# Six Strassen pairs in the last two blocks, activation tables loaded at launch, one state copy split over two engines, and a reordered head

## The chip, the cores and the metric

The kernel runs on one core of one Trainium2 chip. The metric is the device time of one launch in microseconds. Every kernel was executed several times, and executions of the kernel before ran on the same chip between them. All executions quoted here are in the fast state with a mean granted clock of 0.99 to 1.00 (the granted clock is the share of its full clock that the tensor engine was given), but for one of 306.76 us of the kernel before, which was slow (over 1.5% above that kernel's fastest) and is left out of the ratios.

## The reference, cut to what matters

```python
def reference(q, k, v, w_in, w_out):        # q, k, v: 8 batches x 8 heads x 576 x 64, f32
    scores = q @ k.transpose(0, 1, 3, 2) / sqrt(64)
    gamma  = 1 - 2.0 ** (-5 - arange(8))                    # one decay per head
    ret    = scores * where(rel >= 0, gamma ** rel, 0)      # rel = i - j
    x      = (ret @ v).transpose(0, 2, 1, 3).reshape(4608, 512)
    h      = x @ w_in                                       # 512 -> 2048
    g      = 0.5 * h * (1 + tanh(c * (h + 0.044715 * h ** 3)))
    return g @ w_out                                        # 2048 -> 512, f32
```

## The kernel before

The retention ("attention") part is computed in chunks of 128 positions, with a running state between chunks. The FFN works in **blocks** of 512 rows. Each of the eight batches gives one block (its first 512 positions), and the last 64 positions of all batches together make a ninth, the tail block. They run in the order 0, 1, 2, 3, 4, 5, 6, tail, 7, so the "last two blocks" are the tail block and block 7. While a block's FFN runs, the attention of the next batch is woven between its matmuls. A block has three parts that matter here. The code below is cut, and cuts are marked.

```python
def bank(name, dt=F32):                       # eight PSUM banks, shared by everything
    return ps.tile([128, 512 if dt == F32 else 1024], dt, tag="bank", name=name)

# inside class Block
def up(self, f):                              # one of 16 columns of 128 of the first FFN
    hp = bank("hp")
    # ... x is xt (tail block) or xb[b]
    for ct in range(4):                       # 4 matmuls of 512, contraction 4 x 128
        nc.tensor.matmul(hp, w_in_sb[:, ct, 128 * f : 128 * f + 128], x[:, :, ct, :],
                         start=(ct == 0), stop=(ct == 3))
    nc.scalar.activation(out=self.g(f // 2)[:, f % 2], in_=hp, func=AF.Gelu_apprx_tanh)

def mix_sa(self, j, n):  # ... three DVE mixes of g: the operands of a Strassen-type
def mix_sc(self, j, n):  # ... second FFN (seven products my, mz, mw, mv, mu, my2, mz2)
def mix_d(self, j, n):   # ... all of them tensor_tensor with both inputs in SBUF, f16

def down(self, m):                            # 16 matmuls of 256, then the sums on DVE or ACT
    self.product(m)
    self.settle(m)
```

The second FFN is thus already done by one Strassen level; the first is not. Around the blocks stand a list of loads, a list of filler matmuls, and one long plan that says behind which unit of PE work each other step is put:

```python
def gelu_table():                             # loads the gelu table, somewhere in the head
    nc.scalar.activation(out=p2[:, 3:4], in_=p2[:, 2:3], func=AF.Gelu_apprx_tanh)

def put(b, n, eng=None):                      # copies the running state n to f16, two halves
    w = att[b]["w", n]
    for hl in range(2):
        copy(eng or nc.scalar, tbd[b % 2][half[hl], n, :, half[hl]], w[half[hl]])

load_qkv(0, 0, 0, "k", None)                  # (batch, half, head group, which, buffer)
load_qkv(0, 0, 0, "q", None)
# ... some 80 further entries, mostly loads of 256 KB, all in one queue: inputs, w_in, w_out, next inputs

pads.update({("tr", 0, 0, 1, 0): 29, ...})    # filler matmuls that keep PE's clock up
plan = add({},
    (0, L(mask)),
    (0, L(tbd_zero, 0, V)),
    (0, L(cast_qk, 0, 0, 0, "k", A)),         # (unit of PE work, step); A, V, G: engine
    (4, L(gelu_table)),
    # ... some 330 further entries
    (78, L(put, 4, 3)),
)
run(units, plan)
```

Of the kernel before, what the change touches and what calls it, by code (L numbers as in the profile page):

```python
# [19 lines left out]
def kernel(  # L20
# [66 lines left out]
    nc.vector.memset(wz, 0.0)  # L87

# [34 lines left out]
    nc.scalar.activation(out=gt, in_=lg[:, 8:12], func=AF.Exp, bias=0.0, scale=128.0)  # L123

# [7 lines left out]

    def gelu_table():
        nc.scalar.activation(out=p2[:, 3:4], in_=p2[:, 2:3], func=AF.Gelu_apprx_tanh)
# [150 lines left out]
    def cast_w_in(g, ct, eng):  # L285
        t = w_raw.pop(("i", g, ct))
        copy(eng, w_in_sb[:, ct, 512 * g : 512 * g + 512], t)
        done(t)

# [162 lines left out]
    def put(b, n, eng=None):  # L452
        w = att[b]["w", n]
        for hl in range(2):
            copy(eng or nc.scalar, tbd[b % 2][half[hl], n, :, half[hl]], w[half[hl]])
# [76 lines left out]
    class Block:  # L532
        def __init__(self, b):
            self.b = b
            self.gT = self.sa = self.sc = self.ost = None
            self.bank = {}
# [23 lines left out]

        def up_half(self, j, u):
# [19 lines left out]
        def mix_sa(self, j, n):  # L581
# [3 lines left out]
            nc.vector.tensor_tensor(  # L585
# [3 lines left out]
        def mix_sc(self, j, n):  # L589
# [3 lines left out]
            nc.vector.tensor_tensor(out=self.sc[:, j : j + n], in0=g[:, :, 0], in1=g[:, :, 1], op=ALU.add)  # L593

        def mix_d(self, j, n):
            g = self.g(j, n)
            nc.vector.tensor_tensor(  # L597
# [133 lines left out]
    def add(plan, *entries):  # L731
# [13 lines left out]
    load_qkv(0, 0, 1, "k", None)  # L745
    load_qkv(0, 0, 1, "q", None)
    load_qkv(0, 0, 0, "v", None)
# [6 lines left out]
    load_qkv(0, 1, 0, "v", None)  # L754
    load_qkv(0, 1, 1, "v", None)
    load_w_in(0, 0, E)
    load_w_in(0, 1, E)
    load_w_in(0, 2, E)
# [4 lines left out]
    load_qkv(1, 0, 1, "q", None)  # L763
    load_qkv(1, 0, 0, "k", None)
    load_w_in(1, 2, E2)
    load_w_in(2, 3, None)
    load_w_in(2, 0, None)
    load_w_in(2, 1, None)
# [3 lines left out]
    load_qkv(1, 0, 0, "v", None)  # L772
    load_w_in(3, 1, None)
    load_w_in(3, 3, None)
    load_qkv(1, 1, 0, "k", O)
    load_w_in(3, 2, None)
    load_qkv(1, 0, 1, "v", None)
    load_qkv(1, 1, 1, "k", O)
    load_qkv(1, 1, 1, "q", O)
# [5 lines left out]
    load_w_out(6, E3)  # L785
    load_w_out(3, None)
    load_w_out(2, None)
# [3 lines left out]
    load_w_out(14, H)  # L791
    load_w_out(13, H)
    load_w_out(7, E3)
    load_w_out(8, O)
    load_w_out(11, H)
    load_w_out(9, O)
# [3 lines left out]
    load_qkv(2, 0, 0, "q", None)  # L800
    load_qkv(2, 1, 0, "k", None)
    load_qkv(2, 0, 0, "k", None)
    load_qkv(2, 1, 0, "q", None)
    load_qkv(2, 0, 0, "v", None)
    load_qkv(2, 0, 1, "k", None)
    load_qkv(2, 0, 1, "q", None)
    load_qkv(3, 0, 1, "k", None)
    load_qkv(2, 0, 1, "v", None)
    load_qkv(2, 1, 1, "k", None)
    load_qkv(2, 1, 0, "v", None)  # L810
    load_qkv(2, 1, 1, "v", None)
    load_tail(0)
    load_qkv(3, 0, 0, "k", None)
    load_qkv(3, 0, 0, "q", None)
    load_qkv(3, 0, 0, "v", None)
# [13 lines left out]
        ("tr", 0, 1, 0, 0): 1,  # L829
        ("tr", 0, 1, 1, 0): 4,  # L830
        ("tr", 0, 1, 1, 1): 5,
        ("st", 0, 1, 0): 0,
        ("st", 0, 1, 1): 6,
        ("us", 0, 0): 0,
        ("us", 0, 1): 11,
        ("xs", 0, 0): 5,
        ("xs", 0, 1): 0,
        ("in", 0, 3): 0,
        ("tr", 0, 0, 0, 0): 5,
        ("tr", 0, 0, 0, 1): 12,  # L840
        ("tr", 0, 0, 1, 0): 29,
        ("tr", 0, 0, 1, 1): 1,
        ("st", 0, 0, 0): 6,
        ("st", 0, 0, 1): 0,
        ("us1", 0, 0): 8,
        ("tr", 0, 1, 0, 1): 8,
        ("in", 0, 1): 10,
        ("us1", 0, 1): 0,
        ("in", 0, 2): 5,
# [6 lines left out]
    def turn():  # L856
# [7 lines left out]
    plan = add({},  # L864
        (0, L(mask)),
        (0, L(tbd_zero, 0, V)),
        (0, L(cast_qk, 0, 0, 0, "k", A)),
        (0, L(cast_qk, 0, 0, 0, "q", V)),
        (4, L(gelu_table)),
        (0, L(tr, 0, 0, 0, 1, S2)),  # L870
        (1, L(score_mm, 0, 0, 0)),
        (0, L(tr, 0, 0, 0, 0, A)),
# [459 lines left out]
```

## Time and profile before

| | kernel before |
|---|---|
| time, median of 3 at first | 302.81 us (302.34 to 303.06) |
| span of the profiled execution | 299.4 us, an execution of 301.22 us |
| PE, DVE, ACT, POOL busy | 97%, 73%, 55%, 27% |
| first batch of 24 up matmuls | starts at 23.43 us |
| span without PE work | 9.7 us, of which 3.4 behind the last matmul |

PE is the tensor engine, PEld its weight load, DVE the vector, ACT the scalar and POOL the GpSimd engine. The page gives busy shares, the windows give each engine's busy time in a stretch, the timeline lists instructions in order with the idle time before them and what ended it. The lines are shown in the prediction below.

### The profile page before, as it was taken

Reading aid. Unit: us, or ns where it says so; the run is one execution under the profiler, and the core shown is the slowest. Engines: PE = TensorE matmul, PEld = TensorE weight load, DVE = VectorE, ACT = ScalarE, POOL = GpSimd, SP = SyncE. Lnnn points to the kernel's source line nnn. Section 1 sums busy time; section 2 is a strip of 40 time slices with the busy share of each in tenths; the row PEclk is TensorE's granted clock in tenths of the full one; section 3 lists DMA queues with packets and bytes.
Section 4 is the critical chain, followed back from the end, with each engine's and each line's share of the span. In section 5 each row is a group of like instructions: output and inputs, shape, how many; then the busy total and the mean of one; then the engine's idle time right before and its main releaser. Section 6 shows DMA issues by size and latency. Waiting matters only on the chain.

```text
span 299.4 us, 8730 instructions
## 1 busy us (share of the span) xinstructions
PE 289.7 (97%) x3700; PEld 205.0 (68%) x3700; DVE 218.2 (73%) x416; ACT 163.3 (55%) x318; POOL 79.7 (27%) x108
## 2 busy tenths in 40 slices
PE   8888999999999999999999999999999999999995
PEld 6775577888885568655875587558755874784484
DVE  4776899999998995899559755975598353543434
ACT  6556888875556782665445544554355226505620
POOL 2663564474240343094046006500000000000000
PEclk9999999999999999999999999999999999999999
DMA  7999999758979999985895999491110021003204
GB/s 207 305 337 330 321 387 317 195 131 209 220 235 217 310 237 220 254 276 108 220 308 152 134 258 267 118 137 25 77 66 2 2 83 59 2 1 76 67 0 142
DMA packets 94711, 52.48 MB, mean 175 GB/s; under 512 B 38352, under 2 KB 88528, under 8 KB 94672
## 3 DMA queue, kind: packets, MB, share of 16 engines
q1 hardware_dynamic: 94336, 51.26, 64.4%
q10 hardware_dynamic: 336, 0.66, 0.8%
q8 instruction: 29, 0.48, 0.6%
q14 instruction: 10, 0.08, 0.1%
HBM read 36.70 MB, written 9.44 MB: 154 GB/s over the span
## 4 chain that ended last, share of the span: by engine, by line
PE 76%; DVE 14%; ACT 6%; DMA 2%; issue 1%; DVEq 0%; ACTq 0%
PE hp L555 32%; PE mz L625 8%; PE my L625 8%; PE mu L625 5%; PE mv L625 5%; PE mw L625 4%; PE xs L467 2%; PE hp L568 2%; PE st L368 2%; DMA ld<-in_k_dram 2%; DVE ret L381 2%; DVE ost L652 2%; PE xs L494 2%; ACT tbd L233 2%; DVE w_out_sb L296 1%; ACT gT L559 1%
## 5 line engine op out<-in xcount | busy, mean ns | idle before, releaser
L559 ACT ACTIVATE gT<-hp 128x512 f16<-128x512 f32 x124 | 73.6, 597 | 63.7 <-PE hp L555 62.9
L555 PE MATMUL hp<-x,w_in_sb 128*128 128x512 f16 x432 | 98.7, 379 | 0.6 <-ACT gT L559 0.5
L555 PEld LDWEIGHTS <-w_in_sb 128*128 128x128 f16 x496 | 47.1, 98 | 52.1 <-issue 1.0
L625 PEld LDWEIGHTS <-gT 128*128 128x128 f16 x576 | 55.8, 98 | 8.0
L381 DVE TENSOR_TENSOR ret<-st,cm 128x512 f16<-128x512 f32 x64 | 40.8, 693 | 2.2 <-PE st L368 2.2
L242 POOL TENSOR_TENSOR cv<-ld,sc 128x512 f16<-128x512 f32 x27 | 30.3, 1133 | 28.6 <-DMA ld<-in_v_dram 16.8
L233 ACT CAST tbd<-ws 64x256 f16<-64x256 f32 x64 | 25.8, 403 | 22.2 <-DVE ws L449 19.4
L233 POOL CAST kq<-ld 128x512 f16<-128x512 f32 x24 | 19.4, 810 | 62.0 <-DMA ld<-in_k_dram 46.0
L593 DVE TENSOR_TENSOR gsum<-gT 128x1024 f16<-128x1024 f16 x36 | 26.7, 740 | 12.3 <-ACT gT L559 12.3
L625 PE MATMUL mz<-w_out_sb,gT 128*128 128x256 f16 x288 | 34.4, 273 | 0.0
L625 PE MATMUL my<-w_out_sb,gT 128*128 128x256 f16 x288 | 34.4, 273 | 0.0
L625 PEld LDWEIGHTS <-gsum 128*128 128x128 f16 x288 | 28.0, 98 | 3.5
L652 DVE TENSOR_TENSOR ost<-ost,mv 128x512 f32<-128x512 f32 x18 | 11.5, 682 | 22.3 <-PE mv L625 19.6
L597 DVE TENSOR_TENSOR gT<-gT 128x1024 f16<-128x1024 f16 x36 | 26.9, 751 | 0.5
L507 DVE TENSOR_TENSOR x<-xs,gx 128x512 f16<-128x512 f32 x32 | 21.8, 685 | 6.5 <-PE xs L494 6.4
L585 DVE TENSOR_TENSOR gdia<-gT 128x512 f16<-128x512 f16 (+1 forms) x34 | 17.9, 527 | 10.1 <-ACT gT L559 7.5
L568 PE MATMUL hp<-x,w_in_sb 128*128 128x256 f16 x160 | 18.9, 273 | 0.8 <-DVE x L507 0.8
L233 ACT CAST kq<-ld 128x512 f16<-128x512 f32 x30 | 18.1, 616 | 1.0 <-DMA ld<-in_q_dram 0.7
L625 PE MATMUL mu<-w_out_sb,gsum 128*128 128x256 f16 x144 | 17.2, 273 | 0.2 <-DVE ret L381 0.2
L625 PE MATMUL mv<-w_out_sb,gsum 128*128 128x256 f16 x144 | 17.2, 273 | 0.0
L625 PE MATMUL mw<-w_out_sb,gdia 128*128 128x256 f16 x144 | 17.2, 273 | 0.0
L568 PEld LDWEIGHTS <-w_in_sb 128*128 128x128 f16 x160 | 15.2, 98 | 2.8 <-issue 0.9
(95 smaller groups left out, 319.8 us busy)
## 6 DMA issues: line engine op xcount, KB each, us to landing
ld<-in_k_dram SPq DMA_DIRECT2D x30, 256.0 KB, 5.3
ld<-in_q_dram SPq DMA_DIRECT2D x30, 256.0 KB, 5.3
ld<-in_v_dram SPq DMA_DIRECT2D x30, 256.0 KB, 5.5
out_dram<-ost SPq DMA_DIRECT2D x14, 512.0 KB, 4.6
loan<-in_moe_w_out_dram SPq DMA_DIRECT2D x12, 256.0 KB, 5.4
loan<-in_moe_w_in_dram SPq DMA_DIRECT2D x8, 256.0 KB, 6.1
ld<-in_moe_w_in_dram SPq DMA_DIRECT2D x8, 256.0 KB, 6.0
ld<-in_moe_w_out_dram SPq DMA_DIRECT2D x4, 256.0 KB, 5.6
```

The source lines that it names most:

```text
L233: (eng.copy if eng is nc.scalar else eng.tensor_copy)(out=out, in_=in_)
L242: eng.tensor_tensor(out=unperm(att[b]["v"][:, s, hh, :]), in0=perm(t), in1=sc[:, 8 * hh : 8 * hh + 8] .rearrange("p (r h) -> p r h", r=2) ...
L381: nc.vector.tensor_tensor(out=x.rearrange("p (a m) -> p a m", a=2), in0=st[hl].rearrange("p (a m) -> p a m", a=2), in1=cm.rearrange("p r s ...
L507: nc.vector.tensor_tensor(out=xb[b][:, :, 2 * s + c].rearrange("p s q i -> p q s i"), in0=att[b]["x", s][c].rearrange("p (q s i) -> p q s ...
L555: nc.tensor.matmul(hp, w_in_sb[:, ct, 128 * f : 128 * f + 128], x[:, :, ct, :], start=(ct == 0), stop=(ct == 3),)
L559: nc.scalar.activation(out=self.g(f // 2)[:, f % 2], in_=hp, func=AF.Gelu_apprx_tanh)
L568: nc.tensor.matmul(hp[:, 256 * h : 256 * h + 256], w_in_sb[:, ct, 256 * j + 128 * h : 256 * j + 128 * h + 128], xb[self.b][:, :, 2 * u : 2 ...
L585: nc.vector.tensor_tensor(out=self.sa[:, j : j + n], in0=g[:, :, 0, 0:256], in1=g[:, :, 1, 256:512], op=ALU.add)
L593: nc.vector.tensor_tensor(out=self.sc[:, j : j + n], in0=g[:, :, 0], in1=g[:, :, 1], op=ALU.add)
L597: nc.vector.tensor_tensor(out=g.rearrange("p j h c -> p j (h c)")[:, :, 256:768].rearrange("p j (h c) -> p j h c", h=2), in0=g[:, :, :, 0: ...
L625: nc.tensor.matmul(o, lhs(j, slice(128 * u, 128 * u + 128)), w_out_sb[:, j, w], start=((u == 0 or isinstance(t, list)) and j == 0 and not ...
L652: nc.vector.tensor_tensor(out=out, in0=in0, in1=t, op=op)
```

## The change

Its intent: take work off PE where PE is the bound, and start it earlier. It has four parts, and the diff is cut to the core of each.

**Strassen pairs.** In the last two blocks, columns 0 and 1, 4 and 5, 8 and 9 are computed in pairs, with seven products in place of eight. The sums of weights are made on POOL, those of x on DVE; ACT and DVE combine the products.

```diff
+        def pair_a(self, j):
+            pv, pw, py = bank("pv"), bank("pw"), bank("py")
+            # ... each mm is two matmuls of 256
+            mm(j, pv[:, 0:256], lambda c: f[:, 2 + c], lambda c: self.x_half(1, 2 + c), True)
+            mm(j, pv[:, 256:512], lambda c: f[:, 4 + c], lambda c: self.x_half(0, c))
+            mm(j, pw[:, 0:256], lambda c: f[:, c], lambda c: self.xf[2][:, c], True)
+            mm(j, py[:, 0:256], lambda c: w[:, c, 0:128], lambda c: self.xf[0][:, c], True)
+            mm(j, py[:, 256:512], lambda c: w[:, 2 + c, 128:256], lambda c: self.xf[1][:, c])
+        # ... pair_q: ACT copies pv, DVE forms four q from py, pw and the copy
+        # pair_b: two further products into py; pair_s: DVE adds them; pair_g: gelu of 1024
+    SP = (0, 2, 4)
...
+                    (21, L(FN.forms_x, "sub0")),
+                    (21, L(FN.forms_x, "sub1")),
+                    (21, L(FN.forms_x, "add")),
+                    (21, L(FN.forms_x, "sum0")),
+                    (21, L(FN.forms_x, "sum1")),
...
+        if t is None or t == B - 1:
+            for j in SP:
+                ups[2 * j : 2 * j + 2] = [L(F.pair_a, j), L(int)]
```

**Tables at launch.** Two one-element activations at the start of the program load exp and then gelu; the call in the plan goes.

```diff
+    nc.scalar.activation(out=p2[:, 3:4], in_=wz[:, 0:1], func=AF.Exp)
...
+    nc.scalar.activation(out=p2[:, 3:4], in_=wz[:, 0:1], func=AF.Gelu_apprx_tanh)
...
-        (4, L(gelu_table)),
```

**State copies.** `put` can send one half to ACT and one to DVE; this is used for the last state of batch 4, which is copied just behind the last product of block 2.

```diff
+            e = (A, V)[hl] if eng is S2 else eng
+            copy(e, tbd[b % 2][half[hl], n, :, half[hl]], w[half[hl]])
...
-        (78, L(put, 4, 3)),
+        (78, L(put, 4, 3, S2)),
```

**Orders.** Some twenty loads change places, the filler counts are set anew, and most plan entries of blocks 0 to 2 move or change engine (ten casts go from ACT or DVE to POOL, six casts of w_in from POOL to ACT or DVE). In blocks 3 to 6 the mixes change order and one mix of each block goes to POOL. A few of the load swaps:

```diff
     load_qkv(0, 0, 1, "k", None)
+    load_qkv(0, 0, 0, "v", None)
     load_qkv(0, 0, 1, "q", None)
-    load_qkv(0, 0, 0, "v", None)
...
     load_w_in(2, 2, None)
-    load_qkv(1, 0, 1, "q", None)
+    load_w_in(1, 2, E2)
     load_qkv(1, 0, 0, "k", None)
-    load_w_in(1, 2, E2)
```

## The prediction

> **What bounds the kernel now.** I read the page first (busy shares, slices, chain), then the windows cut at the first up-projection and at the borders between up and down, then the timeline of the head and of the last border. The page's busy shares, and two rows of its slices:
>
> ```profile
> PE 289.7 (97%) x3700; PEld 205.0 (68%) x3700; DVE 218.2 (73%) x416; ACT 163.3 (55%) x318; POOL 79.7 (27%) x108
> PE   8888999999999999999999999999999999999995
> PEclk9999999999999999999999999999999999999999
> ```
>
> PE is busy 97% of the span at full clock, so a saving must take work off PE, or idle time and filler. The windows (columns: stretch, its length, then busy us and count of PE, PE weight load, DVE, ACT, POOL, then clock, DMA share, GB/s) say where the idle time is:
>
> ```profile
> 0.00:20.56 20.56, 17.26 (x356) 14.25 (x357) 13.99 (x44) 11.58 (x23) 10.09 (x25) 1.00 0.95 278
> 20.56:43.27 22.71, 21.25 (x245) 13.72 (x245) 18.07 (x31) 17.05 (x34) 11.58 (x16) 1.00 1.09 343
> 43.27:64.98 21.71, 21.10 (x296) 18.05 (x294) 21.20 (x42) 19.82 (x45) 12.96 (x12) 1.00 0.84 234
> 64.98:91.68 26.70, 26.54 (x494) 22.69 (x494) 26.42 (x51) 12.55 (x28) 10.16 (x14) 1.00 0.84 215
> ...
> 243.88:257.69 13.81, 13.81 (x67) 6.32 (x65) 5.66 (x10) 8.96 (x15) 0.00 (x0) 1.00 0.20 78
> 257.69:269.92 12.23, 12.23 (x114) 10.91 (x112) 4.98 (x8) 2.37 (x4) 0.00 (x0) 1.00 0.00 1
> 269.92:283.73 13.81, 13.81 (x67) 6.28 (x65) 5.67 (x10) 8.74 (x15) 0.00 (x0) 1.00 0.30 77
> ```
>
> Of 9.7 us without PE work, 3.3 lie before 20.56 us, 1.5 up to 43 us, 0.8 up to 92 us, 3.4 behind the last matmul. From 142 us on PE never rests. In the last two blocks, where the Strassen pairs go, DVE is busy 5.7 of 13.8 us, ACT about 9, POOL 0: there is room beside PE. Between 43 and 92 us DVE is busy 47.6 of 48.4 us, a second bound there. The head's 17.26 us of PE are mostly filler: 16 warm-up matmuls (3.59 us) and 116 pads of about 56 ns (6.5 us). The head is a chain of latencies, and this is where the old table load sits (timeline of ACT):
>
> ```profile
> 10.16 0.59 ACT L233 COPY T<-tr 128x512 f16<-128x512 f16 x1 [2.21 <-PE tr L315]
> 10.76 1.28 ACT L134 ACT_TABLE_LOAD   x1
> 12.05 0.20 ACT L134 ACTIVATE p<-p 128x1 f32<-128x1 f32 x1
> 13.02 0.82 ACT L233 CAST tbd<-ws 64x256 f16<-64x256 f32 x2 [0.77 <-DVE ws L449]
> 13.87 0.62 ACT L233 CAST kq<-ld 128x512 f16<-128x512 f32 x1
> ```
>
> The cast at 13.87 releases two transposes and so on to the first up-projections; behind the state copies, it starts later than its data.
>
> **What the Trainium skill says.** "TensorE: Matmul & The Clock Gate", section "Back-to-back issue gap", gives N/2.4 + 2.5 ns for the isolated gap: 216 ns at N=512, 109 at N=256. Its sustained figure of 131 ns for N=512 does not fit this trace: 64 up matmuls take 13.81 us, 216 ns each, and 16 down matmuls of 256 columns 1.75 us, 109 ns each, each with its own weight load of 98 ns hidden beside it. I use the trace. "ScalarE: Activation LUTs", section "What ACT_TABLE_LOAD costs", has 1283 ns for the load and 1380 ns of drain per switch; the trace shows 1.28 us, and no drain of that size (the next ACTIVATE starts at once). "SBUF — State Buffer", section "Who interferes with whom": a DVE instruction with two SBUF inputs contends with a GpSimd instruction that reads SBUF, and the loser waits for the whole instruction. The trace is in line with it without proving it: L597 on DVE (both inputs SBUF) takes 0.60 to 0.69 us while POOL is idle, and 751 ns in the mean.
>
> **The change part by part.**
>
> 1. Strassen. A pair of columns took 8 matmuls of 512: 8 x 215.8 = 1.726 us. Now it takes 4 into pv, 2 into pw, 4 + 4 into py, 14 of 256: 14 x 109.3 = 1.530 us. Saved 0.196 us a pair, 1.18 us for six, all on the engine that sets the end. Weight loads rise from 8 to 14, 98 ns each under 109 ns, as in the down-projection.
> Added beside it, per pair: an ACT copy of 512 (0.59 us); on DVE one op of 512 from PSUM (0.69), two of 256 (0.42 each) and another of 512 (0.69), 2.2 us; one gelu of 1024 in place of two of 512. For a block DVE goes from 5.7 us to about 5.7 + 6.6 - 3.2 (five mixes move to POOL) + 1.7 (five forms of x, f16, about 0.34 us each) = 10.8 of 13.2 us. ACT gains about 1.5 us and stays near 10.5. POOL gets five mixes of 1024 f16; its two-input op of 512 takes 1.04 us alone, so I estimate 2.1 us each, 10.5 us a block. All below PE.
> The twelve weight forms go to POOL in block 7's attention stage (214 to 244 us), where it was idle: twelve ops of 256 or 512, an estimated 8 us in 30.
> Border to the first Strassen block, the only tight one. In the old trace the tail of xt is made at 241.5 to 242.8 us, the my product settled by 243.3, and PE leaves the old block at 243.7. The five forms now follow that settle: the third, which pw needs, ends at about 243.3 + 3 x 0.34 = 244.3, and PE arrives after four pv matmuls at 244.2. A stall of 0.1 to 0.3 us. The mz settle then waits for the last form (245.0 to 245.7), q follows to 246.4, and PE reaches its second batch at 246.8: no stall. The built program shows that pw and py get banks of mw and mv, already free, so the late mz settle does not block them. The last block's forms are made a block ahead: no stall. A DVE mix held up to 2 us by a POOL mix would delay the later pairs; by the same walk those have 0.5 to 1.5 us to spare, so I take 0.1 us.
> Net of part 1: 1.18 - 0.2 - 0.1 = 0.9 us.
>
> 2. Head. Both table loads now stand at launch: exp from about 1.0 to 2.3 us, gelu behind the last exp from 4.45 to 5.75. ACT is then free for the first copy of T at 5.95, about when q is transposed. The 1.48 us at 10.76 go away. The first casts move to POOL behind a zeroing of 1.9 us, q ends at 5.4 and k at 6.0 us instead of 5.2 both, so the first scores come at about 7.1 in place of 7.4. v of head group 0 is loaded fourth in place of fifth; the state product still waits for v of group 1 (seventh load, landing 9.97 + 1.04 of POOL). The casts of the second half leave ACT for POOL and no longer stand behind the state copies. The last q load, landing at 14.2, becomes the limit: cast 14.8, transpose 15.2, copies to 16.4, last scores 16.5 in place of 17.94. The masks wait on v, load 14 in place of 13, about 16.5 by the 0.7 us between landings here; then values end about 19.2 in place of 20.56. The second batch of up matmuls, at 23.43 in the old trace, starts about 22.0. Gain at this point: 1.4 us.
>
> 3. What is left of it. Up to 43 us the DMA moves 343 GB/s with its engines full, so weights and block 1's inputs do not come earlier because PE does; from 43 to 92 us DVE is full with unchanged work. Some casts of block 1 leave DVE (about 2 us by 43 us, where it has 4.6 us idle), which helps. I keep 0.9 of the 1.4 us. The other moves of mixes and casts through blocks 2 to 7 act where PE has no idle time: 0.
>
> 4. State copies. Only four keep both engines or move to DVE: put of the third state of block 0 goes to DVE, and the last put of block 4 is split over ACT and DVE. The wait before the first gelu of block 4 was 0.51 us (timeline at 126.3), of which 0.1 is counted here.
>
> Sum: 0.9 + 0.9 + 0.1 = 1.9 us; 302.81 - 1.9 = 300.9 us.
>
> **The rivals.** (a) The head's gain is lost: the DMA, at 1.09 share up to 43 us, and the full DVE after it set the time at 92 us whatever the head does. For it: these two windows. Against: PE itself is busy 94 to 99% there, so it is no less a bound. Result about 301.8. (b) POOL becomes the bound of the last blocks: 1024-wide mixes of more than 3 us under contention, so that mv waits for the last sum on POOL and my2 for the last difference. For it: POOL casts in the old trace stretch to 3.4 us at 55 us under a busy DVE. Against: the last sum has 5.2 us from the end of up, the last difference 8.7. It would cost up to 1 us a block, about 302.5. (c) The whole head gain stays and the new order of casts also takes most of the 2.3 us that PE idles between 20 and 92 us. For it: so many reordered entries look like a search that kept what was faster. Against: no wait in that stretch is longer than 0.8 us. About 299.5.
>
> **Range and chances.** The centre 300.9 has part 1 at 0.9 (0.5 to 1.2) and the head at 1.0 (0 to 2.2). The ends: low 299.6 with rival (c), high 302.3 with (a) and some of (b). Faster by over 2% needs 6.1 us: all PE idle time but the tail is 6.3 us, so beyond reach without cutting filler too, 0.03. Slower by over 2% would need a stall in every block: 0.02. Within 2%: 0.95.
>
> **What would show it.** Right: up windows of the last two blocks of about 13.3 and 13.2 us in place of 13.81; first hp matmul about 1.2 us earlier than 20.5, the 24-fold batch near 22.0; block borders at 92 us about 0.9 us earlier and those from 142 on by a constant amount; one PE gap of 0.1 to 0.3 us at the first pw. Wrong: py or hp waiting for DVE or ACT in the last blocks, gsum from POOL releasing mv, new PE gaps on ACT casts of w_in between 22 and 36 us, or an unchanged time at 92 us.

## The result, and the profile after

The kernel after took 298.89 us in the median of four executions (298.35 to 299.75), the kernel before 302.72 us in the same rounds (302.34 to 303.06). The ratio is 0.9877, with a 95% interval of 0.9848 to 0.9906. A ratio here is the mean time of one kernel's fast executions over that of the other's in the same rounds, so it is not quite the ratio of the medians. The class "within 2%" was right, but the time lies below the predicted range of 299.6 to 302.3: the gain was about twice the 1.9 us expected.

Busy shares of the kernel after, and two rows of its slices, from its page:

```profile
PE 289.5 (97%) x3748; PEld 208.9 (70%) x3748; DVE 234.3 (79%) x434; ACT 161.9 (54%) x316; POOL 121.6 (41%) x142
...
PE   8989999999999999999999999999999999999995
...
PEclk9999999999999999999999999999999999999999
```

PE is still the bound at full clock. DVE and POOL are busy 16 and 42 us longer than before, and the kernel is faster all the same. The windows of the kernel after, cut at the same events as those of before (columns as there):

```profile
0.00:20.05 20.05, 18.00 (x377) 15.37 (x378) 12.62 (x40) 10.37 (x22) 12.53 (x30) 1.00 0.93 269
20.05:42.93 22.88, 21.20 (x239) 13.13 (x236) 17.81 (x32) 17.30 (x35) 13.06 (x17) 1.00 1.08 329
42.93:63.76 20.83, 20.83 (x296) 17.91 (x294) 20.07 (x42) 18.75 (x44) 10.79 (x11) 1.00 0.94 271
63.76:90.91 27.15, 26.82 (x494) 22.80 (x494) 26.87 (x51) 12.45 (x29) 13.15 (x17) 1.00 0.89 218
...
242.65:256.36 13.71, 13.55 (x86) 8.10 (x84) 11.56 (x23) 9.55 (x15) 6.56 (x3) 1.00 0.20 79
256.36:268.59 12.23, 12.23 (x115) 10.96 (x113) 10.14 (x14) 2.46 (x5) 4.48 (x2) 1.00 0.01 1
268.59:281.81 13.22, 13.22 (x84) 8.01 (x83) 9.88 (x17) 9.06 (x15) 6.56 (x3) 1.00 0.30 79
```

The up-projection of block 7 now takes 13.22 us in place of 13.81, without idle time; that of the tail block 13.71, with 0.16 us idle. In this trace the 0.5 us won before the first up-projection (20.05 in place of 20.56) grow only to 0.8 at 91 us (90.91 in place of 91.68).

The two traces first taken, 299.4 and 297.5 us, differ by 1.9 us, which is what was predicted. The medians differ by 3.8 us. So the first question is how much one trace says. The kernels were run again, unchanged, and I compare the start of the same matmul in all traces. "Batch" is the first batch of 24 up matmuls, "block n" the first matmul of the first down product (my) of block n. (Block 6 is the one before the tail block and the seventh to run; an expectation that says block 7 in that place means it.)

| trace, us | batch | block 0 | block 2 | block 3 | block 6 | block 7 | span |
|---|---|---|---|---|---|---|---|
| before | 23.43 | 57.81 | 110.06 | 141.73 | 231.08 | 283.57 | 299.4 |
| before, again | 23.67 | 58.71 | 111.97 | 143.64 | 233.00 | 285.48 | 301.3 |
| after | 22.72 | 57.12 | 109.30 | 140.66 | 230.01 | 281.64 | 297.5 |
| after, again | 22.12 | 56.35 | 108.42 | 139.40 | 228.75 | 280.38 | 296.2 |
| after, third | 23.23 | 57.32 | 109.30 | 140.27 | 229.63 | 281.25 | 297.1 |

Two things are to be seen. The two traces of before differ by 1.9 us, all of it before block 2; from there on they run in step. And the means of the two kernels differ as follows: 0.86 us at the batch (23.55 less 22.69), 1.15 more up to block 2, 0.57 from block 2 to block 3 (31.67 less 31.10), 0.0 from block 3 to block 6 (89.35 in each), and 0.86 from block 6 to block 7 (52.49 less 51.63). The sum is 3.4 us, the difference of the mean spans.

Two traces against three are few for the first two of these terms. Some of the runs below are, up to block 2, the same program as the kernel before (strassen_only, put_split) or as the kernel after (no_strassen twice, add_first). With them, four traces stand against six, and the new program leads by 0.7 us at the batch (23.50 less 22.82), by 0.6 at block 0, and by 1.2 at block 2 (110.81 less 109.62, where the two groups still overlap: 110.06 to 111.97 and 108.42 to 110.68). So the lead up to block 2 is 1 to 2 us by the traces, and the timed runs have to say more.

### The profile page after: what moved, and what is told of

Same layout as the page of the kernel before. It is cut to its first block, busy times and chain, and to the rows that moved or that the text cites. A ratio compares the mean times of both kernels' runs of the same rounds, so it can differ in the third digit from the quotient of the medians.

```text
span 297.5 us, 8910 instructions
## 1 busy us (share of the span) xinstructions
PE 289.5 (97%) x3748; PEld 208.9 (70%) x3748; DVE 234.3 (79%) x434; ACT 161.9 (54%) x316; POOL 121.6 (41%) x142
## 4 chain that ended last, share of the span: by engine, by line
PE 74%; DVE 13%; DMA 4%; SPq 4%; issue 2%; ACT 2%; DVEq 0%; ACTq 0%
PE hp L583 27%; PE my L726 9%; PE mz L726 9%; PE hp L669 5%; PE mw L726 5%; PE mu L726 4%; PE mv L726 4%; SPq L188 3%; DVE ret L408 3%; DMA loan<-in_moe_w_in_dram 2%; DMA ld<-in_moe_w_in_dram 2%; PE xs L495 2%; DVE gT L698 2%; DVE ost L753 2%; PE xs L522 2%
## 5 line engine op out<-in xcount | busy, mean ns | idle before, releaser
L583 PE MATMUL hp<-x,w_in_sb 128*128 128x512 f16 x408 | 94.1, 379 | 0.2 <-DVE ret L408 0.2
L587 ACT ACTIVATE gT<-hp 128x512 f16<-128x512 f32 x112 | 65.9, 598 | 42.3 <-PE hp L583 40.4
L583 PEld LDWEIGHTS <-w_in_sb 128*128 128x128 f16 x448 | 42.5, 98 | 44.9 <-issue 0.8
L241 POOL TENSOR_TENSOR cv<-ld,sc 128x512 f16<-128x512 f32 x28 | 31.4, 1136 | 28.8 <-DMA ld<-in_v_dram 26.0
L232 POOL CAST kq<-ld 128x512 f16<-128x512 f32 x31 | 20.7, 677 | 51.8 <-DMA ld<-in_k_dram 26.3
L232 ACT CAST tbd<-ws 64x256 f16<-64x256 f32 x61 | 24.6, 403 | 24.7 <-DVE ws L476 21.3
L698 DVE TENSOR_TENSOR gT<-gT 128x1024 f16<-128x1024 f16 x30 | 28.5, 955 | 0.2
L694 DVE TENSOR_TENSOR gsum<-gT 128x1024 f16<-128x1024 f16 x32 | 23.4, 730 | 2.7 <-ACT gT L656 2.7
L686 DVE TENSOR_TENSOR gdia<-gT 128x512 f16<-128x512 f16 (+1 forms) x30 | 22.5, 751 | 2.4 <-ACT gT L587 2.1
L694 POOL TENSOR_TENSOR gsum<-gT 128x1024 f16<-128x1024 f16 x4 | 8.9, 2223 | 35.1 <-ACT gT L656 32.2
L669 PEld LDWEIGHTS <-w_in_sb 128*128 128x128 f16 x160 | 15.2, 98 | 3.4 <-issue 1.0
```

The lines of the kernel that those rows point to most:

```text
L232: (eng.copy if eng is nc.scalar else eng.tensor_copy)(out=out, in_=in_)
L241: eng.tensor_tensor(out=unperm(att[b]["v"][:, s, hh, :]), in0=perm(t), in1=sc[:, 8 * hh : 8 * hh + 8] .rearrange("p (r h) -> p r h", r=2) ...
L669: nc.tensor.matmul(hp[:, 256 * h : 256 * h + 256], w_in_sb[:, ct, 256 * j + 128 * h : 256 * j + 128 * h + 128], xb[self.b][:, :, 2 * u : 2 ...
L686: e.tensor_tensor(out=self.sa[:, j : j + n], in0=g[:, :, 0, 0:256], in1=g[:, :, 1, 256:512], op=ALU.add)
L694: e.tensor_tensor(out=self.sc[:, j : j + n], in0=g[:, :, 0], in1=g[:, :, 1], op=ALU.add)
L698: e.tensor_tensor(out=g.rearrange("p j h c -> p j (h c)")[:, :, 256:768].rearrange("p j (h c) -> p j h c", h=2), in0=g[:, :, :, 0:256], in ...
```

## The experiments

Each ratio is against executions of the kernel before on the same chip. All results were correct.

### Both kernels again: b_again, a_again, a_third

No edit.

> The kernel before, unchanged, for a second profile. Theory L (the profile of before that was read fell in a lucky execution: its device time was 301.22 us, outside the 302.34 to 303.06 us of the timed runs): the new executions have device times of 302.3 to 303.1 us, spans of about 300.6 to 301.3 us, and the new trace shows the extra 1.2 to 1.9 us in one stretch before 142 us, most likely in the DMA-fed part up to 45 us. Theory P (profiling itself makes before faster by 1.5 us): again a profiled execution near 301.2 us beside timed ones of 302.7 us.

> The changed kernel, unchanged. Ratio to before 0.985 to 0.990. If its executions spread less than those of before in the first 45 us, the change removed a variable wait; theory L expects its new trace to show the first batch of 24 up matmuls within 0.3 us of 22.7 us again, while the new trace of before has it later than 23.4 us.

> The changed kernel again: 2.8 to 3.8 us faster than before, as in the first two measurements; from the traces' stretches 0.8 us (pairs) + 0.5 us (state copies) + 1.7 us (up to block 2's down-projection) = 3.0 us.

The kernel before against itself gave 301.97 against 301.73 us, ratio 1.0016 (0.9981 to 1.0051). The kernel after gave 298.91 us with 0.9917 (0.9885 to 0.9949) against the same executions, and in its third set 298.95 us with 0.9882 (0.9853 to 0.9911). Over all sets, 58 fast executions of the kernel before have a median of 302.22 us (300.71 to 304.66), and 14 of the kernel after 298.95 us (298.00 to 299.78). Only 7 of the 58 were below 301.3 us, and the execution that I had taken the trace from, of 301.22 us, was as fast as those. Theory P is out: this time the profiled execution was the slowest of its four (303.07 us). Theory L held in the main, but not in its details: the four new executions spread from 301.20 to 303.07 us instead of lying at 302.3 or more, the extra 1.9 us came bit by bit between 23 and 112 us, and the batch of the kernel after was not fixed at 22.7 us (22.12 and 23.23 in the further traces). **The gain is about 3.3 us, and the base of my prediction mixed two things: durations from a fast execution and the median of slower ones.** The 3.8 us of the first set are 0.5 more, because the kernel before was a little slow in it.

### The pairs alone: strassen_only

```diff
+        def pair_a(self, j): ...        # and pair_q, pair_b, pair_s, pair_g, forms_w, forms_x
...
+        ups = [L(F.up, f) for f in range(NF)]
+        if t is None or t == B - 1:
+            for j in SP:
+                ups[2 * j : 2 * j + 2] = [L(F.pair_a, j), L(int)]
```

Applied to the kernel before, with the plan of the last two blocks and nothing else.

> The kernel before plus the Strassen pairs alone (old launch, loads, pads, order of the first five blocks and of the loop). Theory of the prediction: 0.9 us faster than before (ratio 0.997), from the traces of before and after 0.86 us between 231 us and the end. Rival: the pairs are worth more in timed runs (1.9 us or more, ratio 0.994 or less).

It took 300.99 us against 301.73, ratio 0.9984 (0.9943 to 1.0026). The timing alone can't tell 0.9 us. The trace can: block 6 to block 7 took 51.54 us in place of 52.49. This stretch was the same within 0.01 us in the two traces of before and in the three of after, so a gain of 0.9 us there is not scatter.

### Everything but the pairs: no_strassen and no_strassen_2

```diff
-            if t is None:
-                add(plan,
-                    (16, L(FL.forms_x, "sub1")),
...
-        if t is None or t == B - 1:
-            for j in SP:
-                ups[2 * j : 2 * j + 2] = [L(F.pair_a, j), L(int)]
```

Applied to the kernel after; the mixes of the last two blocks go back to DVE.

> The changed kernel without the Strassen pairs and their forms, with all mixes of the last two blocks on VectorE as before. Theory of the prediction: 1.0 us faster than before (ratio 0.9967). If the gain beyond the prediction lies in the order of the first blocks (theory L), it is 2.5 to 3 us faster (ratio about 0.991), and strassen_only and no_strassen together give the whole 3.8 us.

> The changed kernel without the pairs, a second time. Its program is that of the changed kernel up to block 7, which the two traces of the changed kernel reach 1.1 and 4.2 us before the two of the kernel before; the first attempt came out at only -0.4 us. If order alone brings the gain beyond the pairs (theory L), the repeat is 2.0 to 2.8 us faster than before (ratio 0.991 to 0.993) and the first attempt was scatter. If it is again within 0.8 us of before, the first 230 us of the changed kernel are not faster by themselves, and something of the pairs acts there.

The first set gave 301.35 us and 0.9989 (0.9947 to 1.0031), the second 299.96 us and 0.9924 (0.9888 to 0.9960). The two sets differ by nearly 2 us for one program on two chips, and their intervals barely meet. Part of this is the reference: in the first set, which was that of a_again too, the kernel before had a median of 301.73 us, 0.5 below that of all sets. I take from it only that something besides the pairs gains, in most executions more than 1 us; the 0.86 us of the pairs rests on the trace.

### Which part of the order: head_new, rest_new, late_new

`head_new` takes the launch, the loads, the fillers and all steps of units 0 to 11 (some 25 us) from the kernel after, and all later steps from the kernel before, without pairs. `rest_new` is the reverse. `late_new` follows the kernel before up to 91 us and has the later steps of the kernel after, with the split copy. A piece of head_new against the kernel after:

```diff
-        (12, L(cast_w_in, 1, 0, G)),
-        (15, L(cast_w_in, 2, 3, G)),
...
+        (12, L(cast_w_in, 1, 0, G)),
+        (14, L(cast_w_in, 2, 3, A)),
+        (12, L(cast_qk, 1, 0, 0, "k", A)),
...
```

> Only the changed kernel's launch, load order, pads and the first 25 us of steps (both tables at launch, casts on GpSimd); all later steps in the order of before, no pairs. Theory of the prediction: the head alone brings 1.4 us at the first batch of 24 up matmuls, of which about 0.9 us is left at the end (ratio 0.997). Theory M (the gain beyond the prediction comes from the later reordering): 0 to 0.5 us.

> Launch, loads, pads and first 25 us as before, then the changed kernel's order and engines of all later steps, no pairs. Theory of the prediction: no change (0 to 0.2 us). Theory M: 1 to 2 us faster (ratio 0.993 to 0.997).

> As before up to 91 us (the first two blocks and their down-projections), then the changed kernel's order for blocks 2 to 7 (split state copy included), no pairs. From the traces: the stretch between the down-projection of block 2 and that of block 3 is 31.67 us in both traces of before and 31.36 and 30.98 us in those of after. So 0.3 to 0.7 us faster (ratio 0.998), all of it in that stretch; theory of the prediction 0.1 us.

head_new took 300.47 us against 302.06, ratio 0.9945 (0.9915 to 0.9976); rest_new 301.61 us, 0.9996 (0.9956 to 1.0036); late_new 302.22 us, 1.0010 (0.9971 to 1.0048). So of everything but the pairs, **1.7 us come with the head and the load order**: 0.55% of the 302.2 us mean of before is 1.66 us. That is nearly twice the 0.9 us that the prediction left of the head, and it is against theory M. The later order shows no gain in time, although in both traces the stretch from block 2 to block 3 is 0.4 to 0.7 us shorter (31.26 and 30.97 in place of 31.67). Each had one execution near 304.6 us, where the kernel before had at most 303.86 in these rounds, and the scatter hides half a microsecond.

late_new's execution of 304.57 us was the profiled one, and shows where such an outlier loses its time. The PE timeline at 22 us, and two windows of it:

```profile
21.93 0.25 PE L496 MATMUL xs<-ret,cv 64*64 64x128 f16 x4 [1.49 <-issue]
```

```profile
18.90:22.30 3.40, 1.89 (x76) 1.39 (x74) 2.71 (x5) 0.54 (x2) 2.73 (x6) 1.00 1.04 324
22.30:25.70 3.40, 2.92 (x21) 2.37 (x20) 0.87 (x2) 0.86 (x2) 1.56 (x3) 0.50 1.00 323
```

PE stood 1.49 us at a place where the first trace of before stood 0.21 us, waiting for nothing that the profile shows. It was thus busy for only 1.89 of 3.40 us, and in the next 3.4 us its granted clock was 0.50. Its batch started at 26.17 us, 2.7 us later than in the first trace of before. What made PE stand is not shown, and I saw this in one trace only.

### The tables alone: launch_only

```diff
+    nc.scalar.activation(out=p2[:, 3:4], in_=wz[:, 0:1], func=AF.Exp)
...
+    nc.scalar.activation(out=p2[:, 3:4], in_=wz[:, 0:1], func=AF.Gelu_apprx_tanh)
...
-        (4, L(gelu_table)),
```

> The kernel before with the activation tables loaded at launch and nothing else changed. Theory T (the removed 1.48 us on ScalarE at 10.8 us is the head's gain): first batch of 24 up matmuls 0.5 us or more before the 23.4 to 23.7 us of the traces of before, total 0.5 to 1.5 us faster. Rival: the head waits elsewhere (casts behind the state copies, masks on v), and the batch moves by less than 0.3 us, total within 0.4 us.

302.86 us against 302.25, ratio 1.0000 (0.9969 to 1.0030), and the batch started at 23.97 us, not earlier than the 23.43 and 23.67 us of before. The load at launch does what it should, as ACT's timeline in the kernel after shows:

```profile
3.99 1.28 ACT L125 ACT_TABLE_LOAD   x1
5.28 0.20 ACT L125 ACTIVATE p<-wz 128x1 f32<-128x1 f16 x1
5.72 0.99 ACT L232 COPY T<-tr 128x512 f16<-128x512 f16 x2 [0.23 <-PE tr L342]
```

The load of 1.28 us ends before ACT's first copy of T has its input. It is free, but the 1.28 us that it leaves in the head were not what the head waited for. Theory T failed: neither the batch nor the time moved as it said.

### The head without its tables, and without its loads: head_old_tables, head_old_loads

```diff
-    nc.scalar.activation(out=p2[:, 3:4], in_=wz[:, 0:1], func=AF.Exp)
...
+        (3, L(gelu_table)),
```

is head_old_tables, against head_new; head_old_loads is head_new with the load list of the kernel before:

```diff
-    load_qkv(0, 0, 0, "v", None)
     load_qkv(0, 0, 1, "q", None)
+    load_qkv(0, 0, 0, "v", None)
...
-    load_w_in(3, 3, None)
     load_w_in(3, 1, None)
+    load_w_in(3, 3, None)
+    load_qkv(1, 1, 0, "k", O)
```

> head_new with the gelu table loaded where the kernel before loads it (before the first state copy) and the exp table by its first user. launch_only showed no gain from the tables. If they matter only beside the new casts: batch at 23.2 us or later, total at most 0.8 us faster than before. If they never matter: batch at 22.6 to 23.0 us, total 1.3 to 1.9 us faster.

> head_new (only the first 25 us of the changed kernel, 1.65 us faster than before) with the load order of before. If the order of the loads brings the gain: first batch of 24 up matmuls at 23.3 us or later, total within 0.4 us of before. If the casts on GpSimd and the pads bring it: batch at 22.6 to 23.0 us, total 1.2 to 1.8 us faster than before.

head_old_tables took 300.73 us against 302.08, ratio 0.9970 (0.9944 to 0.9995), with the batch at 22.77 us and block 2 at 109.37, close to head_new (22.71 and 108.94); its gain in time is 0.9 us where head_new's was 1.7, with overlapping intervals. This lies between the two outcomes expected, so the time leaves open whether the tables are worth some tenths beside the new head; the batch, at 22.77 beside 22.71, doesn't show it. head_old_loads took 302.61 us, ratio 1.0008 (0.9980 to 1.0036). Its batch started at 22.84 us, so the head's lead was there, but block 0 came at 58.97 us in place of head_new's 56.74, and block 2 at 112.00. **With the old load order the new head's lead at 23 us is worth nothing.** The intervals of head_new and head_old_loads don't overlap. (The profiled execution of head_old_loads was its slowest, 303.08 us, and that of head_new one of its fastest, 300.14 us, so their traces lie further apart than their medians.) The timeline of head_old_loads shows where the lead begins to go:

```profile
25.96 0.43 DVE L232 CAST w_in_sb<-ld 128x512 f16<-128x512 f32 x1 [2.50 <-DMA ld<-in_moe_w_in_dram]
...
27.69 0.82 ACT L232 CAST tbd<-ws 64x256 f16<-64x256 f32 x2 [1.10 <-DVE ws L476]
...
29.55 0.61 ACT L232 CAST w_in_sb<-ld 128x512 f16<-128x512 f32 x1
...
30.21 0.39 PE L583 MATMUL hp<-x,w_in_sb 128*128 128x512 f16 x1 [0.27 <-ACT w_in_sb L232]
...
33.97 0.63 ACT L232 COPY T<-tr 128x512 f16<-128x512 f16 x1
...
34.65 0.42 PE L395 MATMUL st<-T 64*64 64x128 f16 x16 [0.97 <-ACT T L232]
```

and that of head_new the same steps:

```profile
24.02 0.43 DVE L232 CAST w_in_sb<-ld 128x512 f16<-128x512 f32 x1 [0.69 <-DMA ld<-in_moe_w_in_dram]
...
27.87 0.61 ACT L232 CAST w_in_sb<-ld 128x512 f16<-128x512 f32 x1
...
32.29 0.63 ACT L232 COPY T<-tr 128x512 f16<-128x512 f16 x1
...
32.97 0.42 PE L395 MATMUL st<-T 64*64 64x128 f16 x16 [0.19 <-ACT T L232]
```

In this trace it begins with a load. DVE waits 2.50 us for a tile of w_in, where in head_new it waits 0.69 us. Behind this cast in DVE's queue stands the scan that makes a state, so ACT waits 1.10 us for that state, and its copy starts at 27.69 us in place of 26.02. ACT's cast of a weight tile then starts 1.68 us later, PE waits for it, and ACT, still late, keeps PE waiting 0.97 us for the copy of T. In the kernel before, this cast of DVE stands behind the scan (at 27.22 us), so the chain shown is what the new head loses when its casts are queued for loads that come in another order; it is not a wait of the kernel before. From a lead difference of 0.13 us at the batch the two kernels are 1.68 us apart at this score product.

### The load order alone: loads_only

```diff
     load_w_in(2, 2, None)
-    load_qkv(1, 0, 1, "q", None)
-    load_qkv(1, 0, 0, "k", None)
     load_w_in(1, 2, E2)
+    load_qkv(1, 0, 0, "k", None)
...
```

The kernel before with the load list of the kernel after, and nothing else.

> The kernel before with only the changed kernel's order of loads. If the loads alone bring it: 1.2 to 1.8 us faster than before. If loads and casts must go together (the loads keep a lead that the casts and pads make): within 0.5 us of before, with the first batch of 24 up matmuls at 23.3 us or later.

Of the two outcomes that I had set against each other, it was the first. It took 301.27 us against 302.76, ratio 0.9953 (0.9923 to 0.9983), which is 1.4 us, and its six executions lay within 0.5 us (301.11 to 301.61) beside 301.56 to 304.66 us of the kernel before's fast ones. So **the load order alone brings most of what the whole head brings**. Its trace alone doesn't say where: batch at 23.14 us, block 2 at 110.34, the latter within the two traces of before. (Its profiled execution took 301.56 us and that of the first trace of before 301.22, so no gain against that trace was to be expected.) PE waited 1.16 us for DVE just ahead of that batch, so the loads alone don't make it as early as the new head does. All traces together say a part of where: from block 0 to block 2, the eight traces with the old list take 52.25 to 53.26 us (mean 52.86), and the ten with the new list 51.89 to 52.70 (mean 52.25); pool_read and pool_write below, which add work there, are left out. The one execution of before at 304.66 us makes 0.2 us of these 1.4.

### One split copy: put_split

```diff
-            copy(eng or nc.scalar, tbd[b % 2][half[hl], n, :, half[hl]], w[half[hl]])
+            e = (nc.scalar, nc.vector)[hl] if eng == 2 else nc.scalar
+            copy(e, tbd[b % 2][half[hl], n, :, half[hl]], w[half[hl]])
...
-        (78, L(put, 4, 3)),
+        (78, L(put, 4, 3, 2)),
```

> The kernel before with only the last state copy of block 4 split over ScalarE and VectorE. From the traces: the stretch between the first down-projection of block 2 and that of block 3 is 31.67 us in three traces with the old order, 31.0 to 31.4 in those with the new. If the split copy removes it: 31.2 to 31.4 us. Rival (the new order of scans and copies does it): 31.6 us. Total within 0.4 us either way.

301.89 us against 302.25, ratio 0.9987 (0.9964 to 1.0010): unclear in time. In the trace the stretch from block 2 to block 3 took 30.98 us. It had taken 31.67 in both traces of before and also in strassen_only, so this is 0.69 us, more than the 0.3 to 0.5 us expected. The timeline of the kernel before at this place:

```profile
123.10 2.52 ACT L233 CAST tbd<-ws 64x256 f16<-64x256 f32 x6 [0.64 <-DVE ws L449]
...
125.64 0.60 ACT L559 ACTIVATE gT<-hp 128x512 f16<-128x512 f32 x1
...
126.29 3.03 PE L555 MATMUL hp<-x,w_in_sb 128*128 128x512 f16 x12 [0.51 <-ACT gT L559]
```

and that of put_split:

```profile
123.16 2.10 ACT L233 CAST tbd<-ws 64x256 f16<-64x256 f32 x5 [0.64 <-DVE ws L449]
...
125.07 0.29 DVE L233 CAST tbd<-ws 64x256 f16<-64x256 f32 x1
125.16 0.59 ACT L560 ACTIVATE gT<-hp 128x512 f16<-128x512 f32 x1
...
125.80 3.54 PE L556 MATMUL hp<-x,w_in_sb 128*128 128x512 f16 x15
```

The first gelu of block 3 starts 0.48 us earlier, and the 0.51 us for which PE waited for it are gone. So are 0.12 us of waiting for a gelu at 127.43 us, the only other wait of PE in this stretch of the first trace of before.

### Reads and writes of POOL beside a full DVE: pool_read, pool_write

From 58 to 115 us DVE is busy 55.05 of 57 us in the first trace of before, and 55.83 in the second. The same DVE instruction takes different times in different traces: the mix at 101 us took 0.68 us in the first, and in the second 1.43 us behind a POOL instruction that had started 0.16 us earlier:

```profile
102.74 1.04 POOL L242 TENSOR_TENSOR cv<-ld,sc 128x512 f16<-128x512 f32 x1 [10.84 <-DMA ld<-in_v_dram]
102.90 1.43 DVE L597 TENSOR_TENSOR gT<-gT 128x1024 f16<-128x1024 f16 x1
```

The Trainium skill's page "SBUF — State Buffer", section "Who interferes with whom", says that a DVE instruction with two SBUF inputs contends with a GpSimd instruction that reads SBUF and not with one that only writes. To see what this is worth to the whole program I added eight POOL steps to the kernel before, at units 45 to 52, once reading SBUF twice and once only writing:

```diff
+    def busy():
+        g = gx.rearrange("p q s i -> p (q s i)")
+        nc.gpsimd.tensor_tensor(out=xt[:, 0, 4:8].rearrange(...), in0=g, in1=g, op=ALU.mult)
+    # pool_write in its place: two memsets of 512 into the same tile
...
+        (45, L(busy)),
+        # ... one at each unit up to 52
```

> The kernel before plus eight GpSimd products of 512 elements that read SBUF twice and write an unused place, spread over 60 to 90 us. Theory D (between 58 and 115 us VectorE is full, and what its two-SBUF-input operations lose behind GpSimd operations that read SBUF comes out of the total): the 105 VectorE instructions between the first diagonal sum of block 0 and the third state of block 3, 65.5 and 68.1 us in the two traces of before against 64.7 us in that of head_new, take 1 to 4 us more, and the total grows by 0.5 to 1.5 us. Rival: the total does not move (within 0.3 us).

> The same eight places, but each with two GpSimd memsets of 512, as long together and reading nothing. Theory D: VectorE loses at most half of what it loses in pool_read, and the total is within 0.4 us of before. Rival (GpSimd's own queue is what delays, by holding back its casts): as slow as pool_read.

pool_read took 304.25 us against 302.25, ratio 1.0055 (1.0032 to 1.0078), or 1.7 us, a little over the 1.5 expected at most; pool_write 302.65 us, 1.0007 (0.9982 to 1.0033), or 0.2 us. The 105 DVE instructions that the expectation names took 69.5 us in pool_read and 64.1 us in pool_write (sums of their durations), beside 65.5 and 68.1 us in the two traces of before. From block 0 to block 2, PE was idle for 2.57 us in pool_read, for 0.78 and 1.24 in the traces of before, and for 0.68 in pool_write. One wait of pool_read makes half of its 2.57 us:

```profile
78.47 1.04 POOL L159 TENSOR_TENSOR xt<-gx 128x512 f16<-128x512 f32 x1
78.77 1.01 DVE L453 TENSOR_TENSOR ws<-vs,gt 128x256 f32<-128x256 f32 x1
...
81.45 0.41 PE L372 MATMUL st<-T 64*64 64x128 f16 x15 [1.22 <-DVE x L511]
```

L159 is one of the added reads. The DVE instruction behind it takes 1.01 us, where it took 0.42 in the second trace of before; with two mixes that are also longer (1.33 and 1.09 us in place of 0.95 and 0.68), DVE starts the x for which PE waits at 80.72 us in place of 79.01, while PE itself is only 0.16 us later; neither trace of before has this wait. So reads added on POOL stretch DVE's instructions with two inputs, and the stretch reaches the end; the added writes hardly do. Three limits: these are single traces, and the profiled execution of pool_write was its fastest, that of pool_read nearly its slowest; and the eight additions are longer in pool_read (POOL is busy for 32.3 us in this window, 29.0 in pool_write and 23.8 before), so that a part of the contrast is due to length and not to reading is not excluded.

### The forms in the order of their use, and reads taken off POOL: add_first, add_first_off

```diff
-                    (21, L(FN.forms_x, "sub0")),
-                    (21, L(FN.forms_x, "sub1")),
                     (21, L(FN.forms_x, "add")),
-                    (21, L(FN.forms_x, "sum0")),
-                    (21, L(FN.forms_x, "sum1")),
+                    (21, L(FN.forms_x, "sub1")),
+                    (21, L(FN.forms_x, "sub0")),
+                    (22, L(FN.forms_x, "sum0")),
+                    (22, L(FN.forms_x, "sum1")),
```

is add_first, against the kernel after. add_first_off adds eight changes of this kind in blocks 0, 2 and 3:

```diff
-        (41, L(cast_qk, 2, 0, 1, "q", G)),
+        (41, L(cast_qk, 2, 0, 1, "q", A)),
...
```

> The changed kernel with the five forms of x for the first Strassen block in another order: the one that pw needs first, the two sums after the mz settle. The traces of the changed kernel have PE idle for 0.3 us or so before pw there. Expected: the stretch from the second my product of block 7 to the first my product of the tail block 16.75 us in place of 17.04 us; total 0.2 to 0.3 us below the 298.9 us of the changed kernel, not to be told from it by time alone.

> add_first with eight casts of blocks 0, 2 and 3 moved from GpSimd to ScalarE, which is busy about 18 of 34 us between 58 and 92 us. Theory D: VectorE loses less behind GpSimd and the total falls 0.3 to 1 us below add_first. Rival: ScalarE's own queue, waiting for the loads of those casts, holds back copies and gelus, and the total grows.

The border to the first pair, in the kernel after:

```profile
242.28 1.75 DVE L609 TENSOR_TENSOR xf<-xt 128x512 f16<-128x512 f16 x5
...
242.65 0.60 PE L613 MATMUL pv<-xt,wf 128*128 128x256 f16 x4
...
243.41 0.39 PE L613 MATMUL pw<-xf,wf 128*128 128x256 f16 x2 [0.16 <-DVE xf L609]
```

and in add_first, where the form that pw needs is made first:

```profile
243.26 1.08 DVE L609 TENSOR_TENSOR xf<-xt 128x512 f16<-128x512 f16 x3
...
243.64 0.60 PE L613 MATMUL pv<-xt,wf 128*128 128x256 f16 x4
244.08 0.38 PE L613 MATMUL pw<-xf,wf 128*128 128x256 f16 x2
```

The wait of 0.16 us before pw is gone, and the stretch from my2 of block 6 to my of the tail block took 16.71 us in place of 17.04. In time this is not to be told: add_first 299.05 us against 302.08, ratio 0.9905 (0.9884 to 0.9926). add_first_off took 299.23 us, 0.9910 (0.9881 to 0.9939), no better. So reads of POOL cost when eight are added to the kernel before, but taking eight off the kernel after gains nothing, against the 0.3 to 1 us expected. Either DVE was not what set the pace there any more, or the casts cost as much on ACT; which of the two is not shown. Neither version beats the kernel after by more than the scatter.

## Why the prediction was wrong, point by point

**What bounds it: right.** PE is 97% busy before and after, and the gain is where it said: idle time of PE ahead of 142 us and work taken off the last two blocks. From block 3 to block 6 nothing changed, as predicted (89.35 us in all five traces of the two kernels).

**Part 1, the pairs: right, in mechanism and size.** Predicted 0.9 us net, measured 0.86. The saving on PE held too. In block 7, whose forms are ready, the stretch from my2 to my went from 17.31 to 16.71 us, 0.60 for three pairs, where 3 x 0.196 is 0.59. In the tail block it was 0.27: the border stall, predicted as 0.2, cost 0.33, which add_first gave back by changing one order. The 0.1 for pairs delayed by POOL did not come, although the collision itself did (a mix of DVE stretched to 2.15 us behind one of POOL of 2.12 at 248.6 us in the trace of after): it fell into slack, as the walk of that part had it. So the two stall terms, 0.2 and 0.1, came out as 0.33 and 0, and their errors cancelled. The load of DVE was sized too low: from the start of the tail block's up-projection to the start of block 7's, DVE was busy for 10.64 us before and 21.70 after, where the prediction's terms add 5.1 us. Most of the excess is its mixes beside POOL's: four of one kind take 1331 ns each in place of 423, and one of another kind 2605 in place of 688. (The prediction's 0.60 us for such a mix with POOL idle is a misreading, too: none of L597 is shorter than 0.68 us.) PE still had no wait there but the one at the border. The forms of the weights took 11.6 us on POOL, not 8, ten of the twelve between 198 and 208 us and so earlier than said; no wait of PE comes from them.

**Part 2, the head: half right, with the wrong cause.** Predicted 1.4 us at the batch, measured 0.86 in the mean of the traces. The prediction began it with the table loads. They are worth nothing measurable: moving them alone left the batch at 23.97 us, and putting them back in the new head left it at 22.77. The early batch comes mostly from the new steps and fillers: with them and the old loads it starts at 22.84 us, with the new loads alone at 23.14. I had followed ACT's queue and had not asked what released the batch: before and after it is DVE's x (0.78 and 0.92 us of waiting), which stands at the end of a chain through PE and DVE.

**Part 3, what is left of it: this is the step that failed.** It said that the weights and block 1's inputs "do not come earlier because PE does", that DVE from 43 to 92 us is full "with unchanged work", and so "I keep 0.9 of the 1.4 us". In fact head and loads are worth 1.7 us at the end (head_new), and the lead did not shrink: 0.86 us at the batch and 2.0 at block 2 in the first five traces, 0.7 and 1.2 in all ten. Past the head I had treated the loads as a fixed stream and valued their new order at 0. A full stream still has an order, and the order decides which cast can run when: with the old order the same head lost its lead between 24 and 35 us, beginning with a cast that waited 2.50 us for its load, and gained nothing (302.61 us); with the new order it gained 1.7 us, and the load order alone 1.4. The fullness of DVE was no fixed amount either. Part of it is waiting for POOL's reads, and eight more of these moved the end by 1.7 us. That this waiting differs from one execution of before to the next I saw in two traces (65.5 and 68.1 us for the same 105 DVE instructions); that it makes their whole difference of 1.9 us is argued, not shown.

**Part 4, the state copies: mechanism right, size off.** "of which 0.1 is counted here" was the term, and it measured 0.69 us in the trace of put_split. I had the wait of 0.51 us before me and discounted it to a fifth for no reason that the trace gave. PE rests at one place behind it, for 0.12 us, and that wait went too; so all of it counts. (What the prediction calls the first gelu of block 4 there is that of block 3, the fourth to run.)

**The base.** I took durations from an execution of 301.22 us and subtracted from a median of 302.81. Compared with that one trace my 1.9 us are exact, and by chance: there 0.7 come by the batch, where 1.4 were predicted. Compared with typical executions the gain is 3.3 us.

**The sum as it came out:** 1.7 us for head and loads (timed), 0.69 for the split copy and 0.86 for the pairs (traces) make 3.2 us, and the three timed sets of the kernel after gave 3.7, 2.5 and 3.6 us (one less the ratio, times 302). Against the 1.9 us expected, 0.8 are missing in part 3 and 0.6 in part 4. Rival (c), which kept the head's gain and added something up to 92 us, was the nearest in its number (299.5 us), but not for its reason: in the first traces PE is idle for 2.2 us between the first up-projection and 92 us before and still for 2.0 after. Rival (b) failed, since POOL's mixes never released a product late. Rival (a), the head's lead lost to what follows, is what head_old_loads does: it was true of the new head with the old load order.

**What stays open.** Which of the load swaps does it, and which waits of the kernel before it removes (the chain shown is that of head_old_loads). Why the first set of no_strassen gained 0.4 us and the second 2.3. How often an execution loses time as that of late_new did, and what PE stood for there.

## What to carry to other kernels

Look whether the profiled execution is a typical one before durations of it are subtracted from a median, and take two traces where the expected gain is under 1%. In this kernel the order of loads in a full queue was part of the critical path, since it set when each cast could start: when a lead at the start is to be kept, check the arrival of each input that the next 20 us need and not only the bandwidth. A wait of the bounding engine with nothing behind it to absorb it counts whole; and a move of two-input work to POOL is to be placed where DVE has slack.

## What the Trainium skill lacked or had wrong

- "TensorE: Matmul & The Clock Gate", section "Back-to-back issue gap": its sustained gap of 131 ns for 512 columns was not seen. 64 matmuls of 512 took 13.81 us, 216 ns each, which is its isolated figure.
- The same page, section "What's actually happening", says that the clock drops after an idle window of about 3.4 us, and gives no busy share at which a window counts as idle. In late_new a stretch of 3.40 us in which PE was busy for 1.89 us, with no gap above 1.49 us, was followed by 3.4 us at a granted clock of 0.50.
- "ScalarE: Activation LUTs", section "What ACT_TABLE_LOAD costs": the load took 1.28 us as stated, but the drain of 1380 ns that it adds was not seen; the ACTIVATE began 0.01 us after the load (3.99 + 1.28, then 5.28).
- "SBUF — State Buffer", section "Who interferes with whom", agrees with the runs (1.43 us in place of 0.68 for a mix behind a read of POOL; 1331 ns in place of 423 for four mixes of the tail block). It lacks what this is worth to a program with a full DVE: eight added reads cost 1.7 us in all, eight pairs of writes 0.2 us.
- No page that I read tells how far the time of a whole program scatters from one execution to the next: 300.71 to 304.66 us over 58 fast executions of the kernel before, and 1.9 us between its two traces, all of it before 112 us of 300.
